# Keeping the low halves of the first four weight chunks in a tile that is not yet in use, in a transformer-like block on one core

## The chip, the core and the metric

The kernel runs on one core of a Trainium2 chip. The metric is the device time of one execution in microseconds; 1107.96 is the median of three runs before the change (1107.52 to 1108.51). The engines are TensorE (PE in the profile; PEld are its weight loads), VectorE (DVE), ScalarE (ACT), GpSimd (POOL) and SyncE (SP), which here issues nearly all DMAs. Each works through its own queue in order and waits on semaphores for the others.

## The reference

Two parts follow each other. The first is an attention in which keys and values are averaged over 8 neighbours (576 positions become 72); the second is a mixing block of a Fourier transform over sequence and channels, a normalization and a feed-forward pair of matrices.

```
q, k, v: (8, 8, 576, 64)     w_ch1: (512, 2048)   w_ch2: (2048, 512)
k_p, v_p = mean of k, v over groups of 8 positions         # 72 of them
attn = softmax(q @ k_p^T / 8);  x = attn @ v_p             # (8, 576, 512)
u = x + real(fft(fft(x, axis=1), axis=2))
un = (u - mean(u)) / sqrt(var(u) + 1e-6)                   # over 512 channels
out = u + relu(un @ w_ch1) @ w_ch2
```

## The kernel before, in words

**Precision.** The large matmuls use operands rounded to fp32r. To keep float32's precision each factor is kept as two tiles, a rounded high part and the low part that is left, and a product is three matmuls: high by high, low by high, high by low.

**Front end.** `fe(b)` (from L231) makes one batch ready: it loads q, k and v, forms scores and softmax, transposes, multiplies by the values, does the Fourier sums as matmuls (psA, psB, psQ, psP), subtracts the mean over channels (L600, tile X) and splits the result into `unh` and `unl`, the centred high and low parts (`centre`, L587; ScalarE L590, VectorE or GpSimd L591). After that come the squares and the variance (L608 on). It is a Python generator of some 29 steps; every `yield` ends one. X is one tile for all batches. `unh` and `unl` are `[128, 4, 1152]`, a ring of two batches: `slot(b)` is column 0 for odd and 576 for even batches.

**Feed-forward.** `ffn` (L661) takes a block of columns and a range of the 16 chunks f of the hidden dimension, 128 hidden units each. Per step (one f) it runs 12 matmuls into g (L687), the ReLU and its low part (hh, L691; hl, L692), and one step later 12 matmuls into four accumulators (acc, L671). `blocks()` (L68) sets the order: batch 0 in two halves of 288 columns with chunks 0 to 7, the same two halves with chunks 8 to 15, then blocks of 384 columns with all 16 chunks, three for two batches, and at last batch 7. These are 208 steps; steps 0 to 7 and 8 to 15 are the first two blocks, both with chunks 0 to 7; batch 1 begins at step 32, and the first block with columns of batch 2 at step 48.

**Weights.** They arrive as float64. `prep_w` (L175) makes one piece (one chunk of one of the two weights): a 512 KB load into a staging tile (`wst`), conversion on ScalarE and VectorE (L190 to L195), a rounded copy to the resident high part (`w1h`, `w2h`, L199), a subtraction on GpSimd in place (L200), and a store of this low part to a tile in device memory (L201, `w1l`, `w2l`). The low parts don't fit on the chip. So for each step `load_low` (L207) brings both back into tiles with tag `w` (L209, L210), of which there are seven, shared with the prepared weights (`wd`) and the last raw ones (`wraw`). A step's loads are emitted at the step before.

```
nc.gpsimd.tensor_tensor(out=d0, in0=d0, in1=raw(wh), op=ALU.subtract)
nc.sync.dma_start(wls[i][:, f, cl], d0)
...
lows[i, n] = t = wk.tile([P, DM], F32R, tag="w", bufs=7, name=f"w{i + 1}low")
nc.sync.dma_start(raw(t), wls[i][:, steps[n]])
```

**What sets the order.** The program is emitted in Python order, and a planner orders each engine's queue by its model of time, earlier emission having the higher priority. Emitted first are batch 0's front end to the centring, 11 weight pieces (`AHEAD`), and all of batch 1's front end with the last steps of batch 0's and ten steps of batch 2's among it (L727 to L739, `STEPS`). Then come the feed-forward blocks. Each has two positions per step, and at every position up to two weight pieces (`need`, L767) and some front-end steps (`advance`, L746) are emitted. For batch 2 that was `(pos + 1) * 20 / 63` steps in all until the step that says "U"; from position `free[b]` on (64 for batch 2, when batch 0's columns are done) one step per position.

Of the kernel before, what the change touches and what calls it, by code (L numbers as in the profile page):

```python
# [14 lines left out]
ALU = mybir.AluOpType  # L15
# [3 lines left out]
B, H, S, D, DM, FF = 8, 8, 576, 64, 512, 2048  # L19
# [22 lines left out]
HZ = {0, 1}  # L42
# [4 lines left out]
UE = [1, 1, 0]  # L47
UL = [3, 3, 2]

AHEAD, LEAD, PACE = 11, 12, 0.65  # L50

THIRD = 18

TAIL0, TAIL1, NEXT, STEPS = 10, 11, 20, 10
E0, O0, E1, O1 = 0, 1, 2, 3

HEADS = [(0, 1), (2, 3), (5, 4), (7, 6)]
# [6 lines left out]
def slot(b):  # L64
    return ((b + 1) % 2) * S
# [10 lines left out]
def raw(ap):  # L76
    return ap.bitcast(F32)
# [3 lines left out]
def tile_kernel(ctx: ExitStack, tc: tile.TileContext, qt, kt, vm, vr, w1, w2, cad, cbd, mkd, out):  # L81
    nc = tc.nc
# [6 lines left out]
    wls = [dp.tile([P, NFC, DM], F32, name=f"w{i + 1}l") for i in range(2)]  # L89
# [21 lines left out]
    unh = cp.tile([P, 4, RING], F32R, name="unh")  # L111
    unl = cp.tile([P, 4, RING], F32R, name="unl")
# [62 lines left out]
    def prep_w(n):  # L175
        if n >= len(pieces):
            return
        i, f, c, w, _ = pieces[n]
        cl = slice(c * P, (c + w) * P)
        if wide:  # L180
            st = staged.pop(n)
            hi = st[:, :, :, 1]
            halves = st.bitcast(U16)
            d0 = wk.tile([P, DM], I32, tag="w", bufs=7, name="wd")[:, 0:w * P]
            di = d0.rearrange("p (c m) -> p c m", m=P)
            dh = d0.bitcast(U16).rearrange("p (c m h) -> p c m h", m=P, h=2)
            d0 = d0.bitcast(F32)

            with tc.issue_after(behind["B", 0].ins) if n == 4 else ExitStack():
                nc.scalar.activation(hi.bitcast(F32), hi.bitcast(F32), AF.Copy, scale=REBIAS)  # L190

                nc.scalar.activation(dh[:, :, :, 0], st.bitcast(U8)[:, :, :, 3], AF.Copy, scale=1.0 / 32.0, bias=-15.5 / 32.0)

            nc.vector.tensor_scalar(out=dh[:, :, :, 1], in0=halves[:, :, :, 3], scalar1=0x8000, scalar2=None, op0=ALU.bitwise_and)  # L194
            nc.vector.scalar_tensor_tensor(out=di, in0=hi, scalar=3, in1=di, op0=ALU.logical_shift_left, op1=ALU.bitwise_or)  # L195
        else:
            d0 = staged.pop(n)
        wh = high(i, f)[:, cl]
        nc.scalar.copy(out=wh, in_=d0)  # L199
        nc.gpsimd.tensor_tensor(out=d0, in0=d0, in1=raw(wh), op=ALU.subtract)  # L200
        nc.sync.dma_start(wls[i][:, f, cl], d0)  # L201
        for m in after.get(n, ()):
            load_w(m)

    lows = {}

    def load_low(i, n):  # L207

        lows[i, n] = t = wk.tile([P, DM], F32R, tag="w", bufs=7, name=f"w{i + 1}low")  # L209
        nc.sync.dma_start(raw(t), wls[i][:, steps[n]])  # L210

    steps = [f for *_, f0, f1 in blocks() for f in range(f0, f1)]
# [18 lines left out]
    def fe(b):  # L231
# [4 lines left out]
        halves = [slice(0, HS), slice(HS, S)]  # L236
# [356 lines left out]
        for cl in halves:  # L593
            ps = bank(b, f"psM{b}")[:, 0:HS]
            if b in NM:
                nc.tensor.matmul(ps, lhsT=raw(avg), rhs=s_[:, cl], start=True, stop=True)
            else:
                nc.tensor.matmul(ps, lhsT=avg, rhs=sh[:, cl], start=True, stop=False)
                nc.tensor.matmul(ps, lhsT=avg, rhs=sl[:, cl], start=False, stop=True)
            nc.vector.tensor_tensor(out=X[:, :, cl], in0=Ub[:, :, cl], in1=ps.unsqueeze(1).broadcast_to([P, 4, HS]), op=ALU.subtract)  # L600
            if b in HZ:
                centre(cl)
        if b not in HZ:
            centre(slice(0, S))
        yield "z"

# [99 lines left out]

    free = {1: 0, 2: 64, 3: 128, 4: 160, 5: 224, 6: 256, 7: 320}
    npre = 20  # L710

    done_w = 0
    fe0, fe1 = fe(0), fe(1)
# [13 lines left out]
    fe2, n2 = fe(2), 0  # L727
    for n, _ in enumerate(fe1):
        if n in (TAIL0, TAIL1):
            next(fe0)  # L730
        if n == TAIL1:
            for _ in fe0:
                pass
        if n >= NEXT and n2 < 8:
            next(fe2)
            n2 += 1
    while n2 < STEPS:
        next(fe2)
        n2 += 1  # L739
    run = {2: [fe2, n2, 0, None]}  # L740

    def start(b, pos):
        if b < B:
            run[b] = [fe(b), 0, pos, None]

    def advance(pos):  # L746
        for b in sorted(run):
            r = run[b]
            if r[3] is None:

                upto = (pos + 1 - r[2]) * (npre / (free[b] - 1) if b == 2 else 1)
            else:
                upto = r[3] + pos - max(free[b], r[2]) + 1 if pos >= free[b] else 0
            while r[1] < upto:
                said = next(r[0], "end")
                r[1] += 1
                if said == "U":
                    r[3] = r[1]
                    r[2] = pos
                    break  # L760
                if said == "free":
                    start(b + 1, pos)
                if said == "end":
                    del run[b]
                    break
# [4 lines left out]
    pos = 0  # L770
# [117 lines left out]
```

## Time and profile before

| | |
|---|---|
| median of three runs | 1107.96 us (1107.52 to 1108.51) |
| profiled execution | 1107.08 us, its span 1105.3 us |
| TensorE busy | 1044.3 us, 94% of the span |
| VectorE, ScalarE, GpSimd busy | 625.3, 419.6, 254.5 us |
| moved by DMA | 175.79 MB, 159 GB/s in the mean |
| loads of low parts | 208 of w1l and 208 of w2l, 256 KB each |

The span is the time from the program's first to its last instruction; the profiled execution's own time is 1.8 us longer. All starts in the profile are counted from the start of the span. Busy time of TensorE counts matmuls with a modelled end, so two neighbours overlap on paper; the time between their starts is what they cost. The granted clock is 1.00 at 2.4 GHz and 0.50 at 1.2 GHz. The view of busy time by stretch has, after the stretch and its length, the busy time of PE, PEld, DVE, ACT and POOL with instruction counts in brackets, then the granted clock, the DMA engines' share and GB/s. A wait is told of the engine that stood idle and of what ended that idle time. A DMA's row shows only its issue; the time to landing stands in the DMA view.

### The profile page before, as it was taken

To read this page: it belongs to the slowest core of one execution; us is meant where nothing else is said; L and a number is where in the kernel's file an instruction comes from. 1 tells how busy PE (TensorE), PEld (TensorE's weight loads), DVE (VectorE), ACT (ScalarE), POOL (GpSimd) and SP (SyncE) were. 2 spreads that over 40 slices of the span, in tenths; PEclk is the share of its full clock that TensorE was granted. 3 is DMA by queue.
4 is the path that set the end of the run, shared out by engine and by line. 5 is a ranking of instruction groups with operands and counts; after the bars stand their busy time and mean duration, and the time that the engine had idled before them with its cause. 6 is when DMAs were issued, how large, how long until landed. Compare 5 with 4: busy or idle time off the path is not lost.

```text
span 1105.3 us, 17483 instructions
## 1 busy us (share of the span) xinstructions
PE 1044.3 (94%) x6484; PEld 1005.3 (91%) x6484; DVE 625.3 (57%) x1228; ACT 419.6 (38%) x1140; POOL 254.5 (23%) x256
## 2 busy tenths in 40 slices
PE   6757898999999999999999999999998999999997
PEld 4545877999999999999999999999997999999997
DVE  7576886856376464755457554755547544532122
ACT  5677864443233331433324332433314422221110
POOL 4474355311140022200322111500223000300000
PEclk8588999999999999999999999999999999999999
DMA  6748987655434453445534544445534334346563
GB/s 224 261 158 260 321 298 229 198 183 160 135 119 151 130 161 124 136 129 153 160 107 141 145 143 147 124 119 166 159 95 127 104 105 123 107 121 187 165 188 98
DMA packets 91877, 175.79 MB, mean 159 GB/s; under 512 B 10128, under 2 KB 17296, under 8 KB 91536
## 3 DMA queue, kind: packets, MB, share of 16 engines
q1 hardware_dynamic: 91504, 172.01, 50.4%
q0 software_dynamic: 288, 2.66, 0.6%
q8 instruction: 51, 0.84, 0.3%
q14 instruction: 34, 0.28, 0.1%
HBM read 156.81 MB, written 17.83 MB: 158 GB/s over the span
## 4 chain that ended last, share of the span: by engine, by line
PE 82%; DVE 7%; DMA 4%; ACT 3%; POOL 1%; issue 1%; SPq 0%; DVEq 0%; POOLq 0%; ACTq 0%
PE acc L671 34%; PE g L687 33%; PE psX L408 3%; PE psA L517 2%; PE psS L327 2%; PE psP L550 2%; PE psB L533 1%; PE psT L365 1%; PE psQ L550 1%; DMA wst<-in_w 1%; DVE unl L591 1%; DVE wd L195 1%; DMA w1low<-w1l 1%; DVE wd L194 1%; DMA w2low<-w2l 1%
## 5 line engine op out<-in xcount | busy, mean ns | idle before, releaser
L692 DVE SCALAR_TENSOR_TENSOR hl<-g,hh 128x384 fp32r<-128x384 f32 (+1 forms) x208 | 108.7, 523 | 207.0 <-ACT hh L691 203.2
L691 ACT ACTIVATE hh<-g 128x384 fp32r<-128x384 f32 (+1 forms) x208 | 96.8, 465 | 316.5 <-PE g L687 305.0
L671 PE MATMUL acc<-hh,w2h 128*128 128x384 f32 (+1 forms) x832 | 190.9, 330 | 4.2 <-DVE U L702 3.6
L671 PE MATMUL acc<-hh,w2low 128*128 128x384 f32 (+1 forms) x832 | 187.3, 327 | 0.0
L687 PE MATMUL g<-unh,w1low 128*128 128x384 f32 (+1 forms) x832 | 178.5, 330 | 4.8 <-DMA w1low<-w1l 4.8
L671 PE MATMUL acc<-hl,w2h 128*128 128x384 f32 (+1 forms) x832 | 179.0, 326 | 2.1 <-DVE hl L692 2.1
L687 PE MATMUL g<-unl,w1h 128*128 128x384 f32 (+1 forms) x832 | 175.6, 328 | 3.8 <-DVE unl L591 3.4
L687 PE MATMUL g<-unh,w1h 128*128 128x384 f32 (+1 forms) x832 | 173.7, 326 | 0.0
L671 PEld LDWEIGHTS acc<-hh,w2h 128*128 128x128 f32 x832 | 142.2, 188 | 7.7 <-ACT hh L691 3.1
L687 PEld LDWEIGHTS g<-unh,w1low 128*128 128x128 f32 x832 | 140.9, 190 | 7.1 <-DMA w1low<-w1l 5.9
L687 PEld LDWEIGHTS g<-unl,w1h 128*128 128x128 f32 x832 | 140.3, 189 | 7.1 <-DVE unl L591 4.9
L671 PEld LDWEIGHTS acc<-hh,w2low 128*128 128x128 f32 x832 | 143.3, 188 | 0.4
L671 PEld LDWEIGHTS acc<-hl,w2h 128*128 128x128 f32 x832 | 140.2, 188 | 3.2 <-DVE hl L692 2.9
L687 PEld LDWEIGHTS g<-unh,w1h 128*128 128x128 f32 x832 | 139.3, 189 | 1.3 <-ACT unh L590 1.0
L344 POOL TENSOR_TENSOR t<-t,sm 128x720 f32<-128x720 f32 x32 | 45.9, 1433 | 283.4 <-DVE sm L343 245.9
L262 POOL TENSOR_TENSOR k<-k 128x288 f32<-128x288 f32 (+1 forms) x56 | 39.9, 712 | 95.2 <-DMA k<-in_kt 87.7
L582 POOL TENSOR_TENSOR U<-X,U 128x576 f32<-128x576 f32 (+1 forms) x16 | 20.9, 1308 | 128.4 <-DVE X L566 128.4
L327 PE MATMUL psS<-kpb,q 128*128 128x144 f32 x280 | 43.9, 292 | 2.6 <-DVE X L600 2.4
L327 PEld LDWEIGHTS psS<-kpb,q 128*128 128x128 f32 x280 | 40.5, 195 | 3.2 <-DVE X L600 2.6
L329 DVE TENSOR_REDUCE mx<-psS 128x6 f32<-128x432 f32 x64 | 33.1, 525 | 11.7 <-PE psS L327 11.4
L340 ACT ACTIVATE t<-t 128x720 f32<-128x720 f32 x28 | 22.5, 803 | 37.1 <-DVE t L338 36.8
L341 DVE TENSOR_REDUCE sm<-t 128x10 f32<-128x720 f32 x28 | 25.2, 899 | 16.7 <-ACT t L340 16.5
(205 smaller groups left out, 1442.6 us busy)
## 6 DMA issues: line engine op xcount, KB each, us to landing
w1low<-w1l SPq DMA_DIRECT2D x208, 256.0 KB, 2.7
w2low<-w2l SPq DMA_DIRECT2D x208, 256.0 KB, 2.8
wst<-in_w SPq DMA_DIRECT2D x30, 512.0 KB, 4.6
q<-in_qt SPq DMA_DIRECT2D x28, 288.0 KB, 3.0
k<-in_kt SPq DMA_DIRECT2D x28, 288.0 KB, 2.9
v<-in_vm SPq DMA_DIRECT2D x28, 256.0 KB, 2.9
out<-U SPq DMA_DIRECT2D x18, 384.0 KB, 3.5
w1l<-wd SPq DMA_DIRECT2D x16, 256.0 KB, 4.5
```

The costliest lines, as they stand in the source:

```text
L262: nc.gpsimd.tensor_tensor(out=out if n == 1 else src[:, :, 0:n], in0=src[:, :, 0] if n == 1 else src[:, :, 0:n], in1=src[:, :, 1] if n == ...
L327: nc.tensor.matmul(ps[:, c * W2J:(c + 1) * W2J], lhsT=q[:, r0:r0 + P], rhs=kpb[g % 2], start=True, stop=True)
L329: nc.vector.tensor_reduce(out=mx[:, c0:c0 + n], in_=pv, op=ALU.max, axis=AX.X, negate=b in SM)
L340: nc.scalar.activation(t, t, AF.Exp, scale=1.0 / 64.0)
L341: nc.vector.tensor_reduce(out=sm, in_=t, op=ALU.add, axis=AX.X)
L344: ins = nc.gpsimd.tensor_tensor(out=t, in0=t, in1=sm.unsqueeze(3).broadcast_to([P, 5, 2, J]), op=ALU.mult)
L408: nc.tensor.matmul(ps, lhsT=w, rhs=a, start=(i == 0), stop=(i == len(mm) - 1))
L550: nc.tensor.matmul(ps, lhsT=w, rhs=a, start=(i == 0), stop=(i == 6))
L671: nc.tensor.matmul(acc[e], lhsT=w[:, e], rhs=h, start=(f == f0 and x == 0), stop=(f == f1 - 1 and x == 2))
L687: nc.tensor.matmul(ps, lhsT=w[:, c], rhs=x[:, ti, cl], start=(n == 0), stop=(n == 11))
L691: nc.scalar.activation(hh, ps, AF.Relu)
L692: nc.vector.scalar_tensor_tensor(out=hl, in0=ps, scalar=0.0, in1=raw(hh), op0=ALU.max, op1=ALU.subtract)
```

## The change

The low parts of chunks 0 to 3 (`FRESH = 4`) are written by GpSimd into the ring's columns 0 to 511 of `unl` (for w1) and `unh` (for w2), plane f. That is batch 1's place. They are still stored to device memory from there. For steps below 16 with f below 4 (steps 0 to 3 and 8 to 11) `load_low` hands out these places and issues no DMA. From step 16 on everything is loaded as before.

Since batch 1's place is taken, its front end stops ahead of the centring: a new `yield` stands after the mean is subtracted, the loop that emits it ends after 26 steps (`UNFOLDED`), and the remaining four (centring, squares, variance, reciprocal root) are emitted at positions 32 to 35 of the feed-forward part (`free[1] = 32`). Batch 2's front end has eight steps ahead of the feed-forward part instead of ten (`STEPS`), stays there until batch 1's is finished, and then gets one step in every second position.

```diff
+FRESH = 4
-TAIL0, TAIL1, NEXT, STEPS = 10, 11, 20, 10
+TAIL0, TAIL1, NEXT, STEPS = 10, 11, 20, 8
+UNFOLDED = 26
...
         nc.scalar.copy(out=wh, in_=d0)
-        nc.gpsimd.tensor_tensor(out=d0, in0=d0, in1=raw(wh), op=ALU.subtract)
-        nc.sync.dma_start(wls[i][:, f, cl], d0)
+        low = fresh(i, f)[:, cl] if f < FRESH else d0
+        nc.gpsimd.tensor_tensor(out=low, in0=d0, in1=raw(wh), op=ALU.subtract)
+        nc.sync.dma_start(wls[i][:, f, cl], raw(low) if f < FRESH else d0)
+        done.add((i, f, c))
...
+    def fresh(i, f):
+        return (unl, unh)[i][:, f, slot(1):slot(1) + DM]
...
     def load_low(i, n):
+        assert any(x[:2] == (i, steps[n]) for x in done)
+        if steps[n] < FRESH and n < 16:
+            lows[i, n] = fresh(i, steps[n])
+            return
...
-            if b in HZ:
+            if b == 0:
                 centre(cl)
-        if b not in HZ:
+        if b == 1:
+            yield
+            for cl in halves:
+                centre(cl)
+        elif b > 1:
             centre(slice(0, S))
...
-    free = {1: 0, 2: 64, 3: 128, 4: 160, 5: 224, 6: 256, 7: 320}
+    free = {1: 32, 2: 64, 3: 128, 4: 160, 5: 224, 6: 256, 7: 320}
...
-        if n >= NEXT and n2 < 8:
+        if n >= NEXT and n2 < STEPS:
             next(fe2)
             n2 += 1
+        if n == UNFOLDED - 1:
+            break
...
-    run = {2: [fe2, n2, 0, None]}
+    run = {1: [fe1, UNFOLDED, 0, UNFOLDED], 2: [fe2, n2, 0, None]}
...
-                upto = (pos + 1 - r[2]) * (npre / (free[b] - 1) if b == 2 else 1)
+                upto = pos + 1 - r[2] if b > 2 else STEPS if 1 in run else r[1] + pos % 2
```

## Rows read from the trace of the kernel before

**Rows 1.** Busy time by stretch, 88 to 330 us.

```profile
88.00:100.00 12.00, 8.28 (x45) 7.93 (x46) 6.77 (x11) 6.60 (x26) 4.59 (x4) 0.65 0.94 309
100.00:150.00 50.00, 46.63 (x299) 39.49 (x299) 41.57 (x83) 40.31 (x119) 19.45 (x17) 1.00 0.94 318
150.00:200.00 50.00, 42.83 (x303) 39.42 (x302) 37.67 (x75) 24.36 (x59) 29.63 (x33) 1.00 0.73 235
200.00:330.00 130.00, 130.00 (x862) 127.73 (x861) 78.78 (x170) 50.55 (x139) 28.71 (x28) 1.00 0.51 157
```

**Rows 2.** TensorE's waits, 77 to 200 us: who was waited for, total, times, longest.

```profile
PE g L687 <- DMA w1low<-w1l: 4.8, 2, 4.2
PE acc L671 <- DVE U L702: 3.0, 3, 1.8
```

**Rows 3.** TensorE in order: start, us, line, operation, tiles [idle before].

```profile
86.39 1.03 PE L386 MATMUL psR<-ident,rt 128*32 128x128 f32 x4 [1.34 <-ACT ah L368]
91.67 2.71 PE L687 MATMUL g<-unh,w1low 128*128 128x288 f32 x8 [4.25 <-DMA w1low<-w1l]
94.17 2.50 PE L327 MATMUL psS<-kpb,q 128*128 128x144 f32 x10
96.40 0.81 PE L671 MATMUL acc<-hh,w2h 128*128 128x288 f32 x4
```

**Rows 4.** SP's DMA issues in order of time, 76 to 100 us.

```profile
87.47 0.33 SPq L210 DMA_DIRECT2D w1low<-w1l  x1
```

**Rows 5.** DMA, 86 to 146 us: totals; issues: count, KB, us to landing.

```profile
DMA packets 8135, 18.49 MB, mean 308 GB/s; under 512 B 928, under 2 KB 928, under 8 KB 8130
...
w1low<-w1l SPq DMA_DIRECT2D x13, 256.0 KB, 4.6
```

**Rows 6.** The same DMA view, 220 to 400 us.

```profile
w1low<-w1l SPq DMA_DIRECT2D x37, 256.0 KB, 2.7
```

**Rows 7.** VectorE in order of time, 72 to 100 us.

```profile
77.64 3.90 DVE L591 TENSOR_TENSOR unl<-X,unh 128x288 fp32r<-128x288 f32 x3
...
90.56 0.68 DVE L195 SCALAR_TENSOR_TENSOR wd<-wst,wd 128x512 int32<-128x512 int32 x1
94.47 1.14 DVE L194 TENSOR_SCALAR wd<-wst 128x512 uint16<-128x512 uint16 x1 [3.23 <-PE g L687]
```

**Rows 8.** Busy time by stretch, as in Rows 1, around the first wait.

```profile
87.00:92.00 5.00, 0.75 (x3) 0.33 (x2) 3.54 (x4) 3.05 (x8) 3.02 (x2) 0.50 0.82 242
...
96.00:98.00 2.00, 2.00 (x16) 2.00 (x15) 1.97 (x6) 0.54 (x2) 0.00 (x0) 0.89 0.98 315
```

**Rows 9.** GpSimd's costliest groups by shape: count, busy us, mean ns.

```profile
L200 POOL TENSOR_TENSOR wd<-wd,w1h 128x512 f32<-128x512 f32 x16 | 20.7, 1295 | 24.6 <-ACT w1h L199 10.9 <-issue 6.4 <-PE acc L671 3.9
...
L591 POOL TENSOR_TENSOR unl<-X,unh 128x576 fp32r<-128x576 f32 x12 | 19.1, 1610 | 21.4 <-ACT unh L590 21.4
```

**Rows 10.** VectorE in order of time, 180 to 210 us.

```profile
181.02 1.19 DVE L702 TENSOR_TENSOR U<-U,acc 128x288 f32<-128x288 f32 x3
...
201.38 1.35 DVE L600 TENSOR_TENSOR X<-U,psM 128x1152 f32<-128x1152 f32 x1
...
204.35 3.54 DVE L591 TENSOR_TENSOR unl<-X,unh 128x288 fp32r<-128x288 f32 x6
```

**Rows 11.** TensorE in order of time, 224 to 230 us.

```profile
228.75 0.65 PE L654 MATMUL psVar<-X,avg 128*128 128x288 f32 x2
```

**Rows 12.** GpSimd in order of time, 312 to 332 us.

```profile
322.69 2.92 POOL L591 TENSOR_TENSOR unl<-X,unh 128x576 fp32r<-128x576 f32 x2 [1.58 <-ACT unh L590]
```

**Rows 13.** TensorE in order of time, 310 to 335 us.

```profile
329.90 0.86 PE L687 MATMUL g<-unl,w1h 128*128 128x384 f32 x4
```

**Rows 14.** SP's DMA issues in order of time, 105 to 124 us.

```profile
116.14 0.42 SPq L210 DMA_DIRECT2D w1low<-w1l  x1
```

**Rows 15.** TensorE in order of time, 120 to 124 us.

```profile
121.41 0.78 PE L687 MATMUL g<-unh,w1low 128*128 128x288 f32 x4
```

**Rows 16.** TensorE's waits, 220 to 1100 us.

```profile
PE psS L327 <- DVE X L600: 2.4, 1, 2.4
```

More of the change, by code (lines that the diff above doesn't have):

```diff
@@ L199, in prep_w @@
         nc.scalar.copy(out=wh, in_=d0)
-        nc.gpsimd.tensor_tensor(out=d0, in0=d0, in1=raw(wh), op=ALU.subtract)
-        nc.sync.dma_start(wls[i][:, f, cl], d0)
+        low = fresh(i, f)[:, cl] if f < FRESH else d0
+        nc.gpsimd.tensor_tensor(out=low, in0=d0, in1=raw(wh), op=ALU.subtract)
+        nc.sync.dma_start(wls[i][:, f, cl], raw(low) if f < FRESH else d0)
+        done.add((i, f, c))
         for m in after.get(n, ()):
             load_w(m)
-    lows = {}
+    lows, done = {}, set()
+    def fresh(i, f):
+        return (unl, unh)[i][:, f, slot(1):slot(1) + DM]
     def load_low(i, n):
+        assert any(x[:2] == (i, steps[n]) for x in done)
+        if steps[n] < FRESH and n < 16:
+            lows[i, n] = fresh(i, steps[n])
+            return
         lows[i, n] = t = wk.tile([P, DM], F32R, tag="w", bufs=7, name=f"w{i + 1}low")
```

## The prediction, made before the changed kernel was run

> **What bounds the kernel now.** I read the busy time by stretch first [rows 1]: from 200 us on TensorE is busy all the time at the full granted clock (130.00 of 130.00 us), so from there the time is its work, and a change gains only what it takes out of the stretch before. There TensorE has holes: 3.72 us of 12 between 88 and 100, 3.37 between 100 and 150, 7.17 between 150 and 200. Then the waits of TensorE [rows 2]: between 77 and 200 us the largest is the first feed-forward matmuls waiting for the reloaded low part of w1, 4.8 us in two waits. The third view, TensorE's instructions around that wait [rows 3], shows the place: batch 1's transposes (psR) start at 86.39, the engine stands idle for 4.25 us, and at 91.67 the eight matmuls with w1low of steps 0 and 1 go. Behind them in the same queue stand ten score matmuls of batch 1 (94.17), and the first second-layer matmul (acc) starts at 96.40. The cause of the wait is a late issue: the first reload is issued by SP only at 87.47 [rows 4], though its data was written long before. The issue is followed by a transfer that is slow because the DMA engines are full: share 0.94 between 88 and 150 [rows 1], a median of 4.6 us from issue to landing in the stretch from 86 to 146, against 2.7 us later [rows 5, 6].
>
> **The change, part by part.**
>
> *The reloads that go.* Chunks 0 to 3, two weights, two blocks: 16 loads of 256 KB, 4.19 MB. All lie between 86 and 146 us, where 18.49 MB move [rows 5]: 23% of that stretch's traffic. For steps 0 and 1 the low parts are in place when the subtraction has run, before batch 0's centred parts are, so the 4.8 us go. What is late next: psR still starts at 86.39 and holds TensorE to about 87.4 (idle of 4.25 ahead of 91.67); the eight w1low matmuls follow, then the evictions hh and hl. VectorE is the one to ask: its queue is full of weight preparation until 90.56 + 0.68 = 91.24 [rows 7]. If hl stays behind that work, acc starts at about 91.7 instead of 96.40, 4.7 us earlier; if the order lets hl in when its input is ready, at about 89 (87.4, some 0.8 for four matmuls and as much for the two evictions), 7.4 us earlier. I take 4.8, the measured wait, near the lower end, because the order of each queue favours weight preparation and the front end over feed-forward.
>
> *The clock.* The granted clock is 0.50 from 87 to 92 us and 0.89 by 96 to 98 [rows 8]: the level 1.2 GHz, after the idle time in front. At that level eight matmuls take 2.5 us (91.67 to 94.17) and the ten score matmuls 2.2 us (94.17 to 96.40, the first acc) [rows 3]. At 2.4 GHz they would take half, 2.35 us less. Some idle time ahead of psR stays, so the clock may fall all the same: bounds 0 and 2.35, I take 1.2, the middle. The Trainium skill, "TensorE: Matmul & The Clock Gate", Part 1 on the clock gate, says that the throttled state is the default and that activity releases it; the trace agrees with the fall. By that rule the whole 2.35 would come back only if TensorE has work through the whole gap, which the sum does not assume.
>
> *The buffers.* Low parts, prepared weights and raw weights share seven buffers (tag w). Of the first 16 steps, eight no longer take two each, and the prepared weight of chunks 0 to 3 gives its buffer back at the subtraction and not at the landing of its store. VectorE's wait of 3.23 us at 94.47, which a first-layer matmul ended [rows 7], is this: a prepared weight could not have its buffer until a low part had been read. It goes. It lies on the weight line, not on TensorE: 0 in the sum; at best it keeps steps 4 to 7 from being late.
>
> *The subtraction to another place.* Eight GpSimd subtractions write fp32r into the centred tiles instead of f32 in place. The row of in-place ones is 1295 ns for 512 columns; the nearest row with an fp32r output is 1610 ns for 576, 1431 for 512 at the same rate [rows 9]. So at most 8 x 0.14 = 1.1 us more of GpSimd, at least none, spread over 50 us in which it has idle time: I take 0. The eight stores to memory remain, same size, from another address.
>
> *The added wait.* Batch 1's centring now writes where the low parts lay, so it must come behind the last matmul of step 11. Queued behind it would be ScalarE's and VectorE's feed-forward evictions. But batch 1's mean is subtracted at 201.38, and the eviction of the second block, whose step 11 is the fourth of eight, starts at 181.02 [rows 10]: some 20 us to spare at least, cost 0. The centring (3.54 us of VectorE for six parts [rows 10]), the squares and the variance are now emitted at positions 32 to 36, the steps 16 to 18, which run before 201 us; only their priority against batch 2's first eight steps falls. Batch 1's first feed-forward step is number 32, sixteen steps later: no wait.
>
> *Batch 2's front end.* Before, ten steps were emitted ahead of the feed-forward part and the rest at 20/63 step per position; now eight ahead, and then one in every second position after batch 1's tail, which brings it to "U" at position 61 instead of 63. From position 64 the rule is the old one. The two steps that move write X, which batch 1's variance matmul reads until 228.75 + 0.65 [rows 11], so they could not run ahead before either: 0, with the rival below.
>
> *What GpSimd and VectorE do to each other.* Three centring subtractions of VectorE took 3.90 us at 77.64, beside GpSimd work [rows 7], while six of the same kind took 3.54 us at 204.35 [rows 10]: 0.7 us more each. Weight subtractions that get their buffer earlier may meet batch 0's centring more often; two such meetings would take back 1.4 us and leave a gain of 4.6. I take none, since the ones that could come earlier wait for raw weights on the full DMA engines. The Trainium skill, "SBUF — State Buffer", SBUF: two separate sides, says that the two engines share a port pair which one instruction holds to its end while the other blocks; the trace agrees with a lengthening.
>
> *Does the gain reach the end?* From 200 us TensorE is full, so an earlier start is kept unless something is late that didn't move. That is batch 2 at step 48: its last low centred part ends at 322.69 + 2.92 = 325.61, and the matmul that reads it starts at 329.90 [rows 12, 13]: 4.3 us of slack. Batch 2 follows batch 1 through X, and batch 1's scores stand behind the wait at 91.67 in TensorE's queue, so its chain moves forward with it. A gain of 6.0 needs a shift of 1.7 us there; I expect it.
>
> *Sum.* 4.8 + 1.2 = 6.0. Profiled execution: 1107.08 us (span 1105.3 and 1.8 around it), giving 1101.1; the median of the runs shown, 1107.96, is 0.88 above it, so 1102.0.
>
> **Rivals.**
>
> 1. *A larger gain.* The reloads pace all of the first two blocks, not only the first wait; with 23% less traffic and free buffers the front end's and the weights' loads come earlier too. For: landing takes 4.6 instead of 2.7 us there. Against: of the waits from 77 to 200 us only those 4.8 us are on a reload, the others on VectorE, ScalarE and GpSimd. TensorE's idle time from 100 to 200 is 10.5 us [rows 1]; half of it more, 5.3, gives 1096.7.
>
> 2. *The wait comes back at chunks 4 to 7.* These still go out and back. Step 6's reload is issued at 116.14 and its matmuls run at 121.41 [rows 14, 15]: with the median landing of 4.6 us there is 0.7 us of slack. If the weight line (raw load, preparation, store, reload) doesn't speed up, block one ends as before and only the clock's part is left: about 1107. Against: step 6's reload waits for a buffer and for the full DMA engines, and both are relieved.
>
> 3. *Slower: batch 2 late at step 48.* The two steps that now come behind batch 1's tail find TensorE and ScalarE full of feed-forward work. From X's release (229.40) to 325.61 the front end takes 96.2 us for 18 steps, 5.3 us a step; two steps late are 10.7 us. It decides from 4.3 us of slip, and at 10.7 the kernel ends 6.4 us later than before, whatever the start gained: 1114.4. The same place two rings later shows that such a wait is real: 2.4 us on batch 6's mean [rows 16]. Against: they are emitted at positions 37 and 39, steps 18 and 19, well ahead of 229 us.
>
> 4. *The change doesn't act*: the order of the queues, planned anew, puts other work in the hole and the first acc starts no earlier. I count it with rival 2.
>
> **Chances.** Forecast 0.56, larger 0.15, no change (2 and 4) 0.15, slower 0.14. A measurement of this kernel tells about 0.2%, 2.2 us, from no change. So faster 0.71, same 0.15, slower 0.14. The forecast's own range is 1099 to 1105.7 (from a gain of 9.0, a little under both upper ends together, 9.75, down to 2.2); the range for 8 in 10 takes in most of the larger gain and the no-change case and cuts the tail of the slower one: 1094 to 1110.
>
> **What would show it.** Right: no TensorE wait on w1low before step 4; first acc near 91 us; clock 1.00 by about 92 us; low loads down from 416 to 400; the end of block two earlier by 5 to 7 us, and the same shift at step 32 and step 48. Wrong: acc at 96 us again (VectorE's order), a wait on w1low at steps 4 to 7, a TensorE wait near 325 us on batch 2's centring, or a shift at 200 us that is gone at 340.

## The result: 0.9% slower, and the profile after

The changed kernel takes 1118.40 us (median of 4 runs, 1116.19 to 1119.18) against 1107.93 (1107.52 to 1108.51) on the same chip: ratio 1.0089, 95% interval 1.0075 to 1.0104. Forecast were 1102.0 and a range of 1094 to 1110. The profiled run took 1116.19 us, its span is 1114.4.

The first part went as predicted, and a little further. TensorE in order of time (start, us, line, operation, tiles, idle before), changed kernel; `unl` and `unh` as second operand are the kept low parts:

```profile
85.81 0.61 PE L400 MATMUL psR<-ident,rt 128*32 128x128 f32 x4 [0.73 <-ACT ah L382]
86.69 0.80 PE L690 MATMUL acc<-hh,w2h 128*128 128x288 f32 x4 [0.27 <-ACT hh L710]
87.33 0.70 PE L690 MATMUL acc<-hh,unh 128*128 128x288 f32 x4
...
91.07 0.90 PE L341 MATMUL psS<-kpb,q 128*128 128x144 f32 x6
```

The first acc matmul starts at 86.69 instead of 96.40 [rows 3], and no wait on w1low is left there. The busy time by stretch (length, then PE, PEld, DVE, ACT, POOL busy, granted clock, DMA share, GB/s) shows what became of it:

```profile
87.00:92.00 5.00, 5.00 (x40) 5.00 (x39) 4.28 (x7) 3.75 (x11) 2.52 (x2) 1.00 0.74 220
88.00:100.00 12.00, 11.91 (x83) 10.69 (x81) 9.35 (x16) 9.90 (x36) 4.75 (x5) 1.00 0.85 279
100.00:150.00 50.00, 43.42 (x253) 36.38 (x253) 39.74 (x80) 38.49 (x110) 21.51 (x19) 0.93 0.87 280
150.00:200.00 50.00, 46.66 (x313) 43.27 (x312) 30.43 (x65) 21.82 (x54) 24.37 (x28) 0.93 0.70 223
200.00:330.00 130.00, 127.36 (x819) 124.38 (x819) 75.28 (x162) 43.89 (x124) 24.55 (x27) 0.97 0.47 141
330.00:345.00 15.00, 12.81 (x64) 11.62 (x64) 14.63 (x26) 8.50 (x18) 6.91 (x5) 0.89 0.48 146
```

Against [rows 1, 8]: from 87 to 92 us TensorE is now always busy at the full clock. But from 100 to 150 it is idler (43.42 us busy for 46.63), from 100 to 200 its clock is 0.93 in the mean where it was 1.00, and behind 200 it is no longer full: 2.64 us idle up to 330, 2.19 from 330 to 345, both with the clock below 1.00. Only from 150 to 200 is it busier (46.66 for 42.83).

To compare kernels I count TensorE's lost time. From the length of a stretch I subtract the work of the matmuls that start in it, each kind at one fixed interval from start to next start (the 40th percentile of that kind in two of the traces, the same for all kernels). What remains is waits and the half clock. All have 6484 matmuls, so the sums differ by what the spans differ, to within 0.6 us. The rows with a letter and a number are the experiments below. Each row is one profiled execution, which lies 2.2 us below the median for the changed kernel and 3.9 us above it for z4, so the sums don't rank the kernels as finely as the medians.

| lost, us | to 100 | 100–140 | 140–200 | 200–250 | 250–350 | 350–end | sum |
|---|---|---|---|---|---|---|---|
| before | 62.3 | 6.8 | 12.1 | 1.0 | 1.2 | 18.4 | 101.8 |
| changed | 54.9 | 12.9 | 10.9 | 6.8 | 6.0 | 19.1 | 110.6 |
| x1 deferral only | 62.9 | 5.8 | 13.0 | 1.4 | 1.4 | 18.6 | 103.1 |
| x2 tail first | 54.8 | 11.4 | 12.1 | 4.6 | 9.2 | 22.1 | 114.2 |
| z1 kept, second block | 64.6 | 6.3 | 10.9 | 1.4 | 4.2 | 20.2 | 107.6 |
| z2 kept, first block | 56.3 | 9.9 | 10.9 | 0.7 | 1.1 | 19.4 | 98.3 |
| z4 first, and w1 in second | 54.8 | 11.0 | 9.8 | 1.3 | 1.1 | 21.9 | 99.9 |
| y9 pieces held | 56.0 | 11.4 | 12.2 | 1.3 | 1.3 | 19.2 | 101.4 |
| x3 two kept, old order | 61.5 | 7.4 | 17.1 | 1.1 | 1.4 | 10.5 | 99.0 |

The start gains 7.4 us (62.3 to 54.9). Of these 6.1 go again from 100 to 140. Then the changed kernel loses 5.8 more than before from 200 to 250 and 4.8 more from 250 to 350. Where these three lie:

*100 to 140.* TensorE's waits, changed kernel, 77 to 200 us (who was waited for, total, times, longest; of the first row 0.8 us and of the last 1.0 us lie between 100 and 140):

```profile
PE g L706 <- DMA w1low<-w1l: 2.5, 3, 0.9
PE g L706 <- DVE hl L711: 2.1, 2, 1.6
PE psVar L655 <- ACT t L350: 2.1, 1, 2.1
PE acc L690 <- DVE U L721: 1.3, 2, 1.0
```

TensorE reaches the work of 110 to 135 us earlier, but what it needs there does not come earlier by as much. Batch 0's variance starts 2.9 us earlier, and the first acc matmul behind block one's eviction 2.8 us later (changed kernel, then before):

```profile
117.42 1.51 PE L655 MATMUL psVar<-avg,X 128*128 128x1 f32 x10 [2.08 <-ACT t L350]
138.30 0.40 PE L690 MATMUL acc<-hh,w2h 128*128 128x288 f32 x1 [1.00 <-DVE U L721]
```

```profile
120.27 1.28 PE L636 MATMUL psVar<-avg,X 128*128 128x1 f32 x10 [1.54 <-ACT t L336]
135.47 0.37 PE L671 MATMUL acc<-hh,w2h 128*128 128x288 f32 x1 [0.93 <-DVE U L702]
```

By stretch, changed kernel and then before:

```profile
100.00:120.00 20.00, 17.02 (x102) 14.17 (x102) 12.72 (x24) 17.11 (x60) 9.03 (x9) 0.96 0.96 302
120.00:140.00 20.00, 16.39 (x103) 14.30 (x102) 19.54 (x41) 14.81 (x36) 7.80 (x6) 0.93 0.77 247
```

```profile
100.00:120.00 20.00, 18.73 (x117) 15.41 (x116) 14.55 (x25) 17.56 (x57) 6.81 (x7) 1.00 0.93 310
120.00:140.00 20.00, 17.90 (x130) 16.94 (x131) 17.65 (x43) 15.48 (x45) 8.39 (x7) 1.00 0.93 310
```

TensorE is idle for 6.6 us in place of 3.4. That is about half of the 6.1 us; most of the rest is the clock, which fell behind two of the waits (0.96 and 0.93 in the mean). VectorE is nearly full from 120 to 140 (19.54 of 20 us, 17.65 before).

*200 to 250.* VectorE in order of time, changed kernel: batch 1's centring comes at 206.90 and its second half at 208.60, 5.5 us later than before (201.38 [rows 10], the second half at 203.1), and now meets block three's eviction and batch 2's al:

```profile
206.90 1.35 DVE L614 TENSOR_TENSOR X<-U,psM 128x1152 f32<-128x1152 f32 x1
...
208.60 1.34 DVE L614 TENSOR_TENSOR X<-U,psM 128x1152 f32<-128x1152 f32 x1
...
209.99 4.59 DVE L605 TENSOR_TENSOR unl<-X,unh 128x288 fp32r<-128x288 f32 x6
214.50 1.18 DVE L720 TENSOR_TENSOR acc<-acc,rb 128x288 f32<-128x288 f32 x3
215.60 0.67 DVE L384 TENSOR_TENSOR al<-psT,ah 128x512 fp32r<-128x512 f32 x1
```

TensorE waits for both, and runs at half speed behind the first wait (0.24 us from acc to acc in place of 0.13; the granted clock is 0.50 from 218 to 223 us):

```profile
216.42 0.41 PE L389 MATMUL psV<-ident,t 128*128 128x128 f32 x2 [1.49 <-DVE al L384]
...
217.39 0.44 PE L690 MATMUL acc<-hh,w2low 128*128 128x288 f32 x1
217.63 0.44 PE L690 MATMUL acc<-hh,w2h 128*128 128x288 f32 x1
...
219.26 0.61 PE L690 MATMUL acc<-hh,w2h 128*128 128x288 f32 x1 [0.95 <-DVE U L721]
```

*250 to 350.* X's last reader runs at 244.12 (228.75 [rows 11]), 15.4 us later:

```profile
244.12 0.65 PE L673 MATMUL psVar<-X,avg 128*128 128x288 f32 x2
```

Batch 2's last low centred part comes 13.9 us later (VectorE's at 338.37 + 1.14 = 339.51, GpSimd's at 338.89, against 325.61 [rows 12]), and TensorE waits for it at step 48, which before had 4.3 us to spare [rows 13]:

```profile
338.37 1.14 DVE L605 TENSOR_TENSOR unl<-X,unh 128x576 fp32r<-128x576 f32 x1
```

```profile
337.68 0.62 PE L706 MATMUL g<-unl,w1h 128*128 128x384 f32 x2 [0.92 <-DVE unl L605]
339.56 0.82 PE L706 MATMUL g<-unl,w1h 128*128 128x384 f32 x3 [1.27 <-DVE unl L605]
```

### The profile page after: what moved, and what is told of

Same layout as the page of the kernel before. It is cut to its first block, busy times and chain, and to the rows that moved or that the text cites. A ratio compares the mean times of both kernels' runs of the same rounds, so it can differ in the third digit from the quotient of the medians.

```text
span 1114.4 us, 17453 instructions
## 1 busy us (share of the span) xinstructions
PE 1053.4 (95%) x6484; PEld 1013.6 (91%) x6484; DVE 624.2 (56%) x1228; ACT 420.7 (38%) x1140; POOL 254.2 (23%) x256
## 4 chain that ended last, share of the span: by engine, by line
PE 79%; DVE 8%; DMA 6%; ACT 2%; POOL 2%; issue 1%; SPq 1%; DVEq 0%; POOLq 0%; ACTq 0%
PE acc L690 33%; PE g L706 33%; PE psX L422 3%; DMA wst<-in_w 3%; PE psS L341 2%; PE psP L564 2%; PE psA L531 2%; DMA v<-in_vm 1%; DVE unl L605 1%; PE psB L547 1%; PE psQ L564 1%; DVE X L614 1%; DVE acc L720 1%; PE psT L379 1%; DMA k<-in_kt 1%
## 5 line engine op out<-in xcount | busy, mean ns | idle before, releaser
L706 PE MATMUL g<-unl,w1h 128*128 128x384 f32 (+1 forms) x832 | 179.7, 330 | 7.0 <-DVE unl L605 6.9
L690 PE MATMUL acc<-hl,w2h 128*128 128x384 f32 (+1 forms) x832 | 182.6, 328 | 0.0
L690 PE MATMUL acc<-hh,w2low 128*128 128x384 f32 (+1 forms) x800 | 181.6, 330 | 0.0
L706 PE MATMUL g<-unh,w1h 128*128 128x384 f32 (+1 forms) x832 | 176.6, 331 | 2.1 <-DVE hl L711 2.1
L706 PE MATMUL g<-unh,w1low 128*128 128x384 f32 (+1 forms) x800 | 172.5, 332 | 2.6 <-DMA w1low<-w1l 2.5
L690 PEld LDWEIGHTS acc<-hh,w2h 128*128 128x128 f32 x832 | 144.8, 191 | 7.0 <-DVE U L721 3.4
L706 PEld LDWEIGHTS g<-unh,w1low 128*128 128x128 f32 x800 | 136.8, 191 | 4.1 <-DMA w1low<-w1l 3.5
L690 PEld LDWEIGHTS acc<-hh,w2low 128*128 128x128 f32 x800 | 139.9, 190 | 0.3
L276 POOL TENSOR_TENSOR k<-k 128x288 f32<-128x288 f32 (+1 forms) x56 | 36.9, 658 | 99.8 <-DMA k<-in_kt 88.8
```

The lines of the kernel that those rows point to most:

```text
L276: nc.gpsimd.tensor_tensor(out=out if n == 1 else src[:, :, 0:n], in0=src[:, :, 0] if n == 1 else src[:, :, 0:n], in1=src[:, :, 1] if n == ...
L690: nc.tensor.matmul(acc[e], lhsT=w[:, e], rhs=h, start=(f == f0 and x == 0), stop=(f == f1 - 1 and x == 2))
L706: nc.tensor.matmul(ps, lhsT=w[:, c], rhs=x[:, ti, cl], start=(n == 0), stop=(n == 11))
```

## The experiments

All are timed against the kernel before on the same chip, whose median was 1108.4 to 1108.6 in every set. "X − mean" with one number is, in the expectations too, the start of the second half of batch 1's centring (1.34 us long; 203.1 before, 208.6 changed).

**First set: is it the new order of the front ends?** Theory A: batch 1's tail falls behind batch 2's first eight steps, and this alone makes X late; and the early start is swallowed at block one's eviction. Theory B: the kept low parts crowd batch 1.

x1_defer_only

```
-FRESH = 4
+FRESH = 0
```

> The new order of the front ends (batch 1's centring and what follows it put behind block one, batch 2's first eight steps ahead of it), with every low part reloaded as before: nothing is kept on chip. Theory A (batch 1's tail falls behind batch 2's first eight steps, and that alone releases X late): X's last reader, the variance matmul at 228.75 us before and 244.1 us in the changed kernel, runs at 240 us or later, batch 2's last centring subtraction ends at 335 us or later (325.6 before, 339.5 changed), and the time is 1114 to 1119. Theory B (the kept low parts crowd the front end with earlier weight work): the reader is at 228 to 234 us and the time is 1107 to 1110. The first acc matmul comes at about 96 us by both.

Measured 1108.83, ratio 1.0003 (0.9992 to 1.0014). X's last reader runs at 231.86. A fell: by themselves the deferral and the new pace of batch 2 cost nothing that can be measured.

x2_tail_first

```
-TAIL0, TAIL1, NEXT, STEPS = 10, 11, 20, 8
+TAIL0, TAIL1, NEXT, STEPS = 10, 11, 20, 5
-    ... STEPS if 1 in run else r[1] + pos % 2
+    ... STEPS if 1 in run else r[1] + (1 if r[1] < 8 else pos % 2)
```

> The whole change, but batch 2's transposes and scores are issued behind batch 1's variance instead of ahead of it. Theory A: X's last reader runs about 10 us earlier than in the changed kernel, at 230 to 235 us, batch 2's last subtraction ends at 326 to 331 us, and the time is 1107 to 1111: the loss goes, and no gain is left, because the early start is lost again at block one's eviction. Theory B: the reader stays at 240 us or later and the time at 1114 or above. By the prediction's own sum, with nothing late at step 48, 1102.

1121.55, 1.0119 (1.0102 to 1.0137). The reader did come earlier (234), but batch 2's transposes then stood behind it and its centring was later still (341.8). X − mean stayed at 208.4: the lateness is older than the tail.

x3_two_kept

```
+        if i == 0 and n < 16 and steps[n] < 2:   # w1 of chunks 0, 1: kept in tile "tail3"
+            lows[i, n] = kept(steps[n])
+            return
```

> The kernel before, with the low parts of w1's chunks 0 and 1 kept on chip in another buffer for steps 0, 1, 8 and 9, and no order of the front ends changed. Theory A: the first acc matmul comes at 87 to 92 us (96.40 before), block one's eviction stays at about 135 us because batch 0's reciprocal root ends it, and the time is 1106 to 1109. By the prediction's own sum (the early start is worth 4.8 us and more at the end when nothing is made late) 1102 to 1104.

1104.73, 0.9965 (0.9950 to 0.9979). That is close to the forecast's number (1102 to 1104), but not for its reason: the first acc came at 88.16, yet by 100 us only 0.8 us was gained (table; step 1's acc came at 97.28), and at 350 it was 5 us behind. It gains after 575 us, most of it at 830 to 850, where a wait of before, on batch 6's centring [rows 16], is gone. The edit also does more than keep two parts: their tile lies in the place (`tail3`) that the rounded w1 of chunks 14 and 15 takes later, and the second of these pieces is done at 172.2 in place of 166.6.

x5_rb_early

```
-TAIL0, TAIL1, NEXT, STEPS = 10, 11, 20, 10
+TAIL0, TAIL1, NEXT, STEPS = 6, 7, 20, 10
```

> The kernel before with batch 0's variance and reciprocal root issued four positions earlier, and nothing else. Theory A: the copy of the reciprocal root, at 132 and 136 us before, comes some 5 us or more earlier; since TensorE reaches block one's last steps only at about 133 us in this kernel, the time moves little, 1104 to 1108. If the reciprocal root already holds block one's end back in the kernel before, 1102 to 1104; if batch 1's chain pays for the earlier issue, 1109 to 1112.

1108.67, 1.0007 (0.9996 to 1.0018): no change. The variance came 17 us earlier, at 103, and X − mean 4.8 us later, at 207.9. So here, in the old order of the front ends, a late batch 1 costs nothing. (The 206.6 that the next set's expectation gives for it is the first half's start.)

**Second set: which use of the kept parts?** Theory C: the early start itself makes batch 1 late. Theory D: the reloads that are gone do.

z1_kept_second_block

```
-        if steps[n] < FRESH and n < 16:
+        if steps[n] < FRESH and 8 <= n < 16:
```

> The whole change, but steps 0 to 3 read their low parts back through DRAM as before and only steps 8 to 11 use the kept ones: eight reloads fewer, and no early start. Theory A (the deferral is to blame) has fallen with x1_defer_only, 1108.83. Theory C now: the early start is to blame, since blocks one and two then run ahead of the weight chunks, and work of batch 1 waits on VectorE and ScalarE behind weight pieces whose raw loads have not landed. By C the first acc matmul stays at about 96 us, batch 1's X - mean ends near 204 us (203.1 before, 208.6 changed) and the time is 1107 to 1110. Theory D (the missing reloads or the buffers that they leave free shift the weight work) has the time at 1113 or above.

1110.80, 1.0022 (1.0012 to 1.0033), X − mean 209.1: slower although nothing starts earlier, and batch 1 as late as in the changed kernel, which speaks against C. The time lies between the two bands.

z2_kept_first_block

```
-        if steps[n] < FRESH and n < 16:
+        if steps[n] < FRESH and n < 8:
```

> The whole change, but only steps 0 to 3 use the kept low parts, and steps 8 to 11 reload theirs: the early start with eight reloads fewer. Theory C: the first acc matmul at about 87 us, step 15's last one ahead of before (168.8 in the changed kernel, 177.6 before), batch 1's X - mean at 207 us or later and 1114 to 1120. Theory D, or a loss that comes from the second block's kept parts: 1104 to 1110.

1103.24, 0.9952 (0.9938 to 0.9965), X − mean 197.1. C fell: with the early start and the whole deferral, but the second block's low parts reloaded, the kernel is faster by 5.3 us. The loss comes with the second block's kept parts. The early start, and behind 200 us the stretches in which the changed kernel lost (from 100 to 140 z2 still loses 9.9 us):

```profile
88.00:100.00 12.00, 12.00 (x81) 11.62 (x81) 8.75 (x16) 9.57 (x31) 4.92 (x4) 0.89 0.85 241
...
200.00:220.00 20.00, 20.00 (x158) 19.89 (x157) 16.30 (x41) 8.27 (x21) 4.13 (x4) 1.00 0.59 178
330.00:345.00 15.00, 15.00 (x94) 14.82 (x93) 11.37 (x23) 6.27 (x14) 0.00 (x0) 1.00 0.54 170
```

x4_two_kept_rb_early and x7_after_rb_early: x5's edit, in x3 and in the changed kernel.

> x3_two_kept (1104.73) with batch 0's variance and reciprocal root issued four positions earlier. If block one's eviction, which waits for the reciprocal root at about 135 us, swallows part of the early start, the first acc of block two comes before 133 us (137.2 in x3_two_kept) and the time falls by 2 us or more, to 1099 to 1103. If the earlier root costs batch 1's chain as much as in x5_rb_early (X - mean at 206.6 for 203.1), 1105 to 1110.

> The whole change with batch 0's variance and reciprocal root issued four positions earlier. In the changed kernel steps 8 to 11 have their hidden values by 135 us and TensorE then waits for block one's eviction, first acc of block two at 138.3. If this stall is what makes the early start worthless, the acc comes at 128 to 133 us and the time is 1106 to 1112. By theory C the blocks only run further ahead of the weight chunks and batch 1's chain is as late or later: 1117 to 1124.

x4: 1105.90, 0.9975 (0.9963 to 0.9987), no better than x3. x7: 1108.58, 1.0000 (0.9987 to 1.0012), 9.8 us less than the changed kernel; the second block's first acc came at 128.16 instead of 138.30. But it lost 11.3 us from 100 to 140 all the same: the eviction is one of several things that wait there.

**Third set: which of the second block's parts, and is it batch 1's place in TensorE's queue?** In the changed kernel the planner puts 24 acc matmuls of steps 8 and 9 ahead of three of batch 1's value passes (theory E).

y8_values_first

```
+   with tc.issue_after(behind["X", 1].ins) if step == 9 else ExitStack():
+       gemm2(f - 1, *prev)          # step 8, behind batch 1's last value matmul
```

> The whole change; block two's acc matmuls of step 8 are issued behind the last of batch 1's value matmuls. TensorE's order is that of the changed kernel up to there; only the place of three value passes and 24 acc matmuls is exchanged. Theory E: with the second block's low parts at hand the planner puts the 24 acc matmuls of steps 8 and 9, which wait for block one's eviction until 138.3 us and then run at the half clock, ahead of batch 1's values, and batch 1's chain pays: last value matmul 151 us (148 before, 143 in z2_kept_first_block), X - mean 208.6 (203.1, 197.1). By E the last value matmul starts at or before 145, X - mean ends at or before 203, and the time is 1101 to 1109. Rival G: what is lost is the TensorE time itself from 125 to 143 us and the order of everything behind, not this place: 1113 to 1119.

1115.76, 1.0066 (1.0045 to 1.0088): in rival G's band. The last value pass started at 143.7, but TensorE lost 5.8 us between the value matmuls: it waited 2.4 us for ScalarE and 1.1 us for VectorE, and ran at the half clock behind that. X − mean was 208.8 again. E fell.

z4_second_block_w1

```
+        if steps[n] < FRESH and (n < 8 or i == 0 and n < 16):
```

> The whole change, but steps 8 to 11 reload w2's low parts and use only w1's kept ones. If it is the kept w1 parts that let block two run ahead of batch 1's work (its first multiplication needs nothing else), the time stays at 1113 to 1119, as in the changed kernel. If w2's kept parts do it (the acc matmuls become ready early), 1101 to 1107, as with the first block's alone (1103.24).

1101.49, 0.9945 (0.9926 to 0.9965), X − mean 198.0: the best of all, by keeping less. Only w2's part of the second block is reloaded.

z5_first_block_rb_early (x5's edit in z2) and x8_two_kept_first (x3 with n < 8)

> z2_kept_first_block (1103.24) with batch 0's variance and reciprocal root issued four positions earlier. If block one's eviction still swallows part of the early start there (first acc of block two at 136.7 us), the time falls to 1098 to 1102. If the earlier root costs batch 1's chain what it cost in x5_rb_early (X - mean 4.8 us later than before), 1105 to 1109.

> x3_two_kept (1104.73: w1's chunks 0 and 1 kept elsewhere, front ends in the old order) with the kept parts used in block one alone. If keeping for the second block is what costs, here too, the time falls to 1101 to 1104. If the second block's kept parts are harmless in the old order, 1104 to 1106.

z5: 1112.13, 1.0023 (1.0004 to 1.0041), above both bands: the same edit that took 9.8 us from the changed kernel added 8.9 to z2. x8: 1103.84, 0.9961 (0.9945 to 0.9976), 0.9 us below x3: in the old order the second block's kept w1 parts cost little or nothing.

**Fourth set: are weight pieces in batch 1's way?** Theory H: with reloads gone the planner draws weight pieces forward. GpSimd's subtraction is the end of a piece. Pieces 24 and 25 in the changed kernel (GpSimd in order of time), and then in the kernel before:

```profile
143.01 1.27 POOL L205 TENSOR_TENSOR wd<-wd,w1h 128x512 f32<-128x512 f32 x1 [0.77 <-ACT w1h L203]
146.08 1.28 POOL L205 TENSOR_TENSOR wd<-wd,w1h 128x512 f32<-128x512 f32 x1 [1.79 <-issue]
```

```profile
152.36 1.26 POOL L200 TENSOR_TENSOR wd<-wd,w1h 128x512 f32<-128x512 f32 x1
157.89 1.29 POOL L200 TENSOR_TENSOR wd<-wd,w1h 128x512 f32<-128x512 f32 x1
```

y9_pieces_held and y10_values_first_pieces_held (the same in y8)

```
+            held = 24 <= n < 28
+            with ... tc.issue_after(behind["R", 1].ins) if held ...:      # ScalarE
+            with tc.issue_after(behind["V", 1].ins) if held ...:          # VectorE
```

> The whole change; four weight pieces (numbers 24 to 27) are held on ScalarE behind batch 1's last R copy and on VectorE behind its last value subtraction. Theory H: the second block's kept w2 parts take away reloads that held "w" buffers, so the planner draws weight pieces forward (piece 24 is done at 144.3 us in the changed kernel, 153.6 before, 148.2 in z4_second_block_w1), and these take VectorE and ScalarE from batch 1's values and what follows. By H X - mean, 208.6 us in the changed kernel, ends at or before 204, and the time is 1100 to 1109. Rival G (the order as a whole, no matter which work stands ahead): 1112 to 1119.

> y8_values_first (1115.76) with the same four weight pieces held. In y8 TensorE lost 5.8 us at 137 to 145 us waiting for ScalarE and VectorE between batch 1's value matmuls, while those engines worked on weight pieces. Theory H: that loss falls to 2 us or less, X - mean (208.8) ends at or before 203 and the time is 1099 to 1108. Rival G: 1111 to 1118.

y9: 1106.06, 0.9972 (0.9958 to 0.9985), 12.3 us less than the changed kernel; X − mean 202.7, and the losses behind 200 us are gone (table). Pieces 24 and 25 in it, and the stretches:

```profile
154.25 2.52 POOL L207 TENSOR_TENSOR wd<-wd,w1h 128x512 f32<-128x512 f32 x2
```

```profile
200.00:220.00 20.00, 20.00 (x154) 19.70 (x153) 18.33 (x35) 10.42 (x27) 4.79 (x4) 1.00 0.55 169
330.00:345.00 15.00, 15.00 (x92) 14.89 (x91) 12.55 (x23) 5.14 (x11) 0.49 (x1) 1.00 0.50 157
```

y10: 1110.33, 1.0010 (0.9998 to 1.0022): 5.4 us less than y8, between the two bands; X − mean 205.0. H said 203.

z8_second_block_w2 and z6_second_block_half_w2

```
+        if steps[n] < FRESH and (n < 8 or i == 1 and n < 16):                        # z8
+        if steps[n] < FRESH and (n < 8 or n < 16 and (i == 0 or steps[n] < 2)):      # z6
```

> The whole change, but steps 8 to 11 reload w1's low parts and use only w2's kept ones: the fourth corner beside none (1103.24), w1 alone (1101.49) and both (1118.40). Theory H as it stands, with w2's part to blame: pieces 24 and 25 done before 146 and 150 us, and the time at 1112 to 1119. If only both together do it (eight reloads fewer, enough free buffers), 1100 to 1106.

> The whole change, but steps 10 and 11 reload w2's low parts: in the second block all of w1 and half of w2 are kept. Theory H in proportion to the reloads that are gone: between w1 alone (1101.49) and both (1118.40), 1106 to 1114. A switch at either end (one order or the other): 1100 to 1104, or 1115 to 1120.

z8: 1110.57, 1.0020 (1.0004 to 1.0035), between the two bands. z6: 1105.73, 0.9966 (0.9954 to 0.9977), just below the proportional band. So what the second block keeps, beside the first's: nothing 1103.24, w1 1101.49, w1 and half of w2 1105.73, w2 alone 1110.57, all 1118.40. The loss goes with w2's part, and is largest with both.

**Last set: the pieces' price elsewhere, and the buffers.** f1_w1_and_held is z4 with y9's hold; f2_six_buffers is the changed kernel with

```
-tag="w", bufs=7
+tag="w", bufs=6
```

> z4_second_block_w1 (1101.49) with the four weight pieces of y9_pieces_held held behind batch 1's values. In z4 pieces 24 and 25 are done at 148.2 and 153.5 us, batch 1's last value matmul starts at 144. If pieces still take time from batch 1 there, the time falls to 1097 to 1101. If z4 has already the order that matters, 1100 to 1104; 1104 or more if later pieces now delay block three.

> The whole change with six "w" buffers in place of seven. Theory H's second half: the reloads that are gone free buffers, and raw loads of weight pieces take them early. With one buffer fewer pieces 24 and 25 are done later than in the changed kernel (144.3, 147.4), at 147 and 151 us or later, X - mean ends at or before 205 (208.6) and the time is 1104 to 1112. If the buffers are not what draws the pieces forward, or if six are too few elsewhere: 1114 to 1125.

f1: 1107.25, 0.9989 (0.9976 to 1.0003). The hold that saved 12.3 us in the changed kernel costs 5.8 in z4, which then loses 13.8 us from 140 to 200 in place of 9.8: TensorE waits 6.9 us there in place of 4.1, longest in sum for the hidden values' low parts (2.9 us, VectorE). That is the third of its bands. f2: 1107.17, 0.9993 (0.9974 to 1.0012), X − mean 201.6. The time is as H said, the pieces are not: piece 24 ends at 145.1 and 25 at 150.1 us, earlier than H's bounds. That freed buffers draw the pieces forward is not shown by it.

**What the times go with.** The 13 kernels with the early start, in order of batch 1's X − mean:

| kernel | piece 24 done, us | X − mean, us | time, us |
|---|---|---|---|
| z2 kept, first block | 152.5 | 197.1 | 1103.24 |
| z4 first, and w1 in second | 148.2 | 198.0 | 1101.49 |
| z6 as z4, and half of w2 | 146.0 | 199.0 | 1105.73 |
| f2 six buffers | 145.1 | 201.6 | 1107.17 |
| f1 z4, pieces held | 154.9 | 202.3 | 1107.25 |
| y9 pieces held | 155.5 | 202.7 | 1106.06 |
| x7 root early | 144.7 | 203.5 | 1108.58 |
| z8 first, and w2 in second | 146.2 | 204.2 | 1110.57 |
| y10 values first, pieces held | 154.7 | 205.0 | 1110.33 |
| z5 z2, root early | 146.7 | 206.7 | 1112.13 |
| x2 tail first | 144.2 | 208.4 | 1121.55 |
| changed | 144.3 | 208.6 | 1118.40 |
| y8 values first | 142.8 | 208.8 | 1115.76 |

The times rise with X − mean almost in order, from 1101 to 1104 us at 197 to 198 up to 1116 to 1122 at 208 to 209. They do not follow piece 24: with that piece at 144 to 146 us the times run from 1105.73 to 1121.55. So an early start is kept as far as batch 1 stays in time. Without the early start this does not hold: x5 has batch 1 late at no cost, and z1 as late as the changed kernel (with piece 24 at 152.0) at 2.3 us.

## Why the prediction was wrong

**"4.8 + 1.2 = 6.0": right, and a little small.** TensorE had lost 7.4 us less by 100 us. The first acc at 86.69 is earlier than both cases weighed (91.7 and 89): psR began at 85.81, not 86.39, and the planner let hl in at 86.70, ahead of the weight preparation. With TensorE busy throughout 87 to 92 the clock stayed at 1.00, so the upper end of the clock's term, 2.35, came: 4.8 + 2.35 = 7.15. By the rule of the Trainium skill that the prediction named ("TensorE: Matmul & The Clock Gate", Part 1), that is the case with work through the whole gap; the trace agrees.

**The terms set at 0.** The subtraction to another place: 1277 and 1274 ns, against 1316 and 1352 in place: 0, right. Port: three centring subtractions beside GpSimd took 3.89 us, as before [rows 7]: right. The added wait: 0, right (step 15's last acc ends at 168.8, and the centring's first write, ScalarE's, starts at 208.28). Batch 2's front end: by itself 0, right (x1, 1.0003). The buffers, "0 in the sum", "at best it keeps steps 4 to 7 from being late": this left something out. With fewer reloads weight pieces came earlier (piece 24 at 144.3 for 153.6 us), and I counted that as harmless or good. In the changed kernel it was not: with four pieces held back (y9) batch 1 is in time and 12.3 us are saved. But early pieces alone do not make batch 1 late (f2 and x7 have them at 145.1 and 144.7, and X − mean at 201.6 and 203.5), so the size of this term stays open.

**"Does the gain reach the end?": the step that failed.** It let batch 1's chain, and batch 2's behind it, move forward with batch 1's scores, and asked only whether the slack of 4.3 us at step 48 would do. What the runs showed in its place: (1) of the gain 6.1 us went again from 100 to 140, about half in waits for work of ScalarE and VectorE that did not come earlier with TensorE, and most of the rest in the clock behind them; the 13 kernels that had lost at most 57 us by 100 lose 9.3 to 12.9 there, those without an early gain 5.8 to 9.5; in z2 and z4 4.5 and 5.4 us are left at 350. (2) Batch 1's chain, from its values on, did not move forward but back, by 5.5 us at its centring. TensorE then waited 2.6 us between 214 and 220 us, the tail, behind batch 2's first steps, came 15.4 us late, and step 48 waited. The deferral, harmless in x1, cost once batch 1 was late.

**Rivals.** Rival 3 named the place (step 48), the rule (slip less 4.3 us) and nearly the amount: 13.9 less 4.3 is 9.6, against 6.4 for two steps. Its cause was wrong: it had two steps moved behind the tail, and x1, which has them, is not slower. Rival 1 (reloads pace more): its time did not come, though weight loads did come earlier, as it said. From 86 to 146 us the traffic fell by 11% (16.38 MB for 18.49 [rows 5]) and not by 23%, since two raw weight loads and two stores more lie in that stretch, and the reloads left landed no sooner (w1's 5.1 us for 4.6). Rival 2: one wait at chunks 4 to 7 came, 0.8 us at step 6; the start was gained all the same. Rival 4: it did act.

**The list of signs.** For the forecast came: no w1low wait before step 4, clock 1.00, 400 low loads, and the end of block two earlier, by 8.8 us (168.8 for 177.6) where 5 to 7 were named. Against it came the wait on w1low at step 6, the wait on batch 2's centring (at 337 to 340 us) and a shift that is gone later: step 31 ends at 249.4 for 249.7.

**What stays open.** Shown is that the loss hangs on the second block's kept w2 parts (z2, z4, z8), and goes when four weight pieces are held back (y9). That it runs through batch 1's lateness is borne out by the order of the 13 kernels, but no run moved batch 1 alone. Not shown is that the pieces are what makes batch 1 late; z1 has it late with piece 24 at 152.0. Rival G, that the planner's whole order from step 8 on came out badly, is not excluded: an earlier root (x7), a smaller pool (f2) and half of w2 reloaded (z6) each undo it too, and the edits of x7 and y9 do harm in z2 and z4 (z5, f1). Kernels with the same early start lie between 1101.5 and 1121.6 us.

## What to carry to other kernels

Where a planner orders the queues, a change of data flow is also a new order: a sum over the old trace holds up to the first place where the queues differ, and what lies behind it needs a range as wide as such orders spread (here 20 us, 1.8%). A stall that is taken away pays only as far as the engine that is busy next; ask at each later stage which chain now gets its turn later, not only which one is earlier. When a change has several uses of one idea, time each use alone: here the half that serves the first block gains 5.3 us, three quarters of it 7.1, and the whole costs 10.5.

## What the runs showed of the hardware that was not expected

Fewer reloads did not make the others land sooner. From 86 to 146 us, 12 low parts came back in place of 26; their median from issue to landing was 5.1 us for w1 and 5.7 us for w2 at 273 GB/s, and 4.6 us for both at 308 GB/s before. In z4, at 275 GB/s, it was 4.4 and 5.3 us.

And a short wait can cost more than itself. The 1.49 us of idle time that end at 216.42 are followed by acc matmuls 0.24 us apart in place of 0.13, with a mean granted clock of 0.93 from 200 to 220 us:

```profile
200.00:220.00 20.00, 17.36 (x122) 16.34 (x122) 18.82 (x35) 9.83 (x25) 7.01 (x8) 0.93 0.45 143
```

Not every such wait does this: in the kernel before, waits of 1.54 us (at 120.27) and 1.83 us (at 182.25) left the clock at 1.00 [rows 1]. What makes the difference, no run here shows.
